# Attention and feed-forward in one kernel on one core: loads reordered, global V rows copied in SBUF, one copy moved to ScalarE

## Chip, cores, metric

The kernel runs on one core of one Trainium2 chip. The metric is device time in microseconds (us). Before the change it is 301.4 us (median; single runs 301.0 to 301.5). A profile is one execution with the hardware profiler; its span, from the first to the last instruction, is about 1.9 us shorter than the time of the same execution. Below, TensorE is PE (PEld its loading of weights), VectorE DVE, ScalarE ACT, GpSimd POOL, SyncE SP.

## The reference

Attention of four batches, eight heads, 768 positions, head dimension 64. A query sees the last 96 keys and the first 8 ("global") keys, with a bias that falls linearly with distance. The result, 3072 rows of 512, goes through a gated feed-forward network with 1536 hidden units. Cut to what matters:

```python
scores = scale * q @ k.T - slope[h] * dist          # dist = 96 for a global key outside the window
a = softmax(where(keep, scores, -1e9))              # keep: global, or 0 <= i - j < 96
x = (a @ v).transpose(0, 2, 1, 3).reshape(B * S, H * D)
g = x @ w_gate
out = (g * sigmoid(g) * (x @ w_val)) @ w_out
```

Inputs and output are float32; what is loaded is kept as fp16, and all the loads that convert are issued from POOL. Below, MB of loads are counted in fp16, as they land.

## The kernel before

Batch 0's attention runs first, alone (the prologue). Then come 8 tiles of 384 tokens; each tile has 12 steps, and each step does one gate and value block of the feed-forward, a quarter of an output block of the tile before, and one of the six steps of a pair of heads of the next batches. The parts that matter:

```python
def load_v(b, c):                  # 7 pieces with 8 rows of room for the global keys in each
    if c < NCH:
        nc.gpsimd.dma_start(out=vS[NG:NG + n, b, c, :, :], in_=v[...])
    else:
        for cc in range(NCH):      # the 8 global rows, once per piece, from DRAM
            nc.gpsimd.dma_start(out=vS[0:NG, b, cc, :, :], in_=v[b, :, 0:NG, :]...)

def transposes(self):              # step 0 of a pair of heads: PE transposes q and k into PSUM
    ...
    nc.scalar.copy(out=self.qT..., in_=trq...)
    for c0, c1, n in (...):        # kT with gaps for the global keys, two instructions
        nc.vector.tensor_copy(out=k3[...], in_=t3[...])
    nc.vector.tensor_copy(out=k3[:, :, 0:NG], ...)
# steps 1 to 3: scores(): matmul, exp on ACT, product with the mask (DVE for batch 0, POOL later)
# steps 4, 5: values(): den and num matmuls, then DVE (batch 0) or ACT, DVE and POOL (later)

stage(0)
load_qk(0, 0, 2); load_qk(0, 2, 4)
for c in range(NCH + 1): load_v(0, c)
load_qk(0, 4, 8)
for g in range(4): load_w(g)
for g in range(3): load_wo(g)
stage(1); load_qk(1, 0, 8)
for c in range(NCH + 1): load_v(1, c)
# ... prologue: batch 0 ...
for t in range(NT):
    for f in range(NFF):
        i = NFF * t + f
        for fn in loads.get(i, []): fn()     # loads of batches 2 and 3
        gate_val(t, f)
        if t > 0: out_part(t - 1, f // 4, f % 4)
        attention(i + AHEAD)                 # AHEAD = 2
```

In the traces POOL's loads stand in program order among its other work. A load issued from POOL takes POOL's time (0.9 us for a large piece of V, see below) and holds back the POOL work behind it.

The softmax here doesn't subtract the row's maximum and nothing guards it: scores larger than these inputs give would overflow.

Of the kernel before, what the change touches and what calls it, by code (L numbers as in the profile page):

```python
# [10 lines left out]
FP16 = mybir.dt.float16  # L11
# [26 lines left out]
def kernel(  # L38
# [12 lines left out]
    nc = tc.nc  # L51

    B, H, S, D = q.shape
    NG, NL = int(n_global), int(n_local)
# [9 lines left out]
    NCH = 7  # L64
# [16 lines left out]
    sb = ctx.enter_context(tc.tile_pool(name="sb", bufs=1))  # L81
# [13 lines left out]
    ones = sb.tile([128, 64], FP16, name="ones")  # L95
    nc.vector.memset(ones, 1.0)
    kTs = [sb.tile([128, NCH * 128], FP16, name=f"kT{i}") for i in range(2)]
    for t in kTs:
        nc.vector.memset(t[:, 6 * 128 + 56:], 0.0)
    vS = sb.tile([128, B, NCH, H, D], FP16, name="vS")  # L100
    nc.vector.memset(vS[:, :, 6, :, :], 0.0)

    qst, kst = {}, {}

    def stage(b):
        qst[b] = sb2.tile([128, H, J * D], FP16, name="qst", tag="qst")
        kst[b] = sb2.tile([128, H, J * D], FP16, name="kst", tag="kst")

    def load_qk(b, h0, h1):
        for st, src in ((qst[b], q), (kst[b], k)):  # L110
            nc.gpsimd.dma_start(  # L111
                out=st[:, h0:h1, :],
                in_=src[b, h0:h1].rearrange("h (p j) d -> p h (j d)", p=128))

    def load_v(b, c):
        if c < NCH:
            n = min(KC, S - KC * c)
            nc.gpsimd.dma_start(  # L118
                out=vS[NG:NG + n, b, c, :, :],
                in_=v[b, :, KC * c:KC * c + n, :].rearrange("h p d -> p h d"))  # L120
        else:
            for cc in range(NCH):
                nc.gpsimd.dma_start(
                    out=vS[0:NG, b, cc, :, :],
                    in_=v[b, :, 0:NG, :].rearrange("h p d -> p h d"))

    wg = sb.tile([128, NC, DFF], FP16, name="wg")
    wv = sb.tile([128, NC, DFF], FP16, name="wv")
# [3 lines left out]
    def load_w(g):  # L132
        f0 = WF * g
        for w, src in ((wg, moe_w_gate), (wv, moe_w_val)):
            nc.gpsimd.dma_start(
                out=w[:, :, f0:f0 + WF],
                in_=src[:, f0:f0 + WF].rearrange("(c p) f -> p c f", p=128))

    def load_wo(g):
        nc.gpsimd.dma_start(  # L140
            out=wo[:, 4 * g:4 * g + 4, :],
            in_=moe_w_out[512 * g:512 * g + 512].rearrange("(f p) d -> p f d", p=128))
# [8 lines left out]
    def bank(name, dt=FP32, cols=512):  # L151
        tags = state["tags"]
        tag = tags[state["n"] % len(tags)]
        state["n"] += 1
        return ps.tile([128, cols], dt, name=name, tag=tag)
# [5 lines left out]
    class Pair:  # L161
# [13 lines left out]
        def transposes(self):  # L175
            b, hp = self.b, self.hp
            trq = bank("trq", FP16, S)
            trk = bank("trk", FP16, S)
            for st, tr in ((qst[b], trq), (kst[b], trk)):
                for j in range(J):  # L180
                    for hi in range(2):
                        nc.tensor.transpose(  # L182
                            tr[64 * hi:64 * hi + 64, 128 * j:128 * j + 128],
                            st[:, 2 * hp + hi, D * j:D * j + D], ident)
            self.qT = sb2.tile([128, S], FP16, name="qT", tag="qT")
            self.kT = kTs[hp % 2]
            nc.scalar.copy(  # L187
                out=self.qT.rearrange("r (p j) -> r p j", j=J),
                in_=trq.rearrange("r (j p) -> r p j", j=J))
            k3 = self.kT.rearrange("r (c m) -> r c m", m=128)  # L190
            t3 = trk.rearrange("r (j p) -> r p j", j=J)
            for c0, c1, n in ((0, 6, KC), (6, 7, S - 6 * KC)):
                nc.vector.tensor_copy(  # L193
                    out=k3[:, c0:c1, NG:NG + n].rearrange("r c (p j) -> r c p j", j=J),
                    in_=t3[:, 20 * c0:20 * c0 + (c1 - c0) * (n // J), :].rearrange(
                        "r (c p) j -> r c p j", c=c1 - c0))
            nc.vector.tensor_copy(  # L197
                out=k3[:, :, 0:NG],
                in_=k3[:, 0, NG:2 * NG].unsqueeze(1).broadcast_to([128, NCH, NG]))
# [22 lines left out]
        def values(self, half, norm):  # L222
            b, hp = self.b, self.hp
            lo, hi_q = HALF[half]
            n_q = hi_q - lo
            num = bank("num")
            den = bank("den")
            parts = []
            for c in range(NCH):
                cb, col, q0, n = chunks[c]  # L230
                a, z = max(q0, lo), min(q0 + n, hi_q)
                if a < z:
                    parts.append((c, cb, col + a - q0, a - lo, z - a))
            for dst, ones_side in ((den, True), (num, False)):
                for i, (c, cb, col, o, n) in enumerate(parts):
                    for hi in range(2):
                        r = slice(64 * hi, 64 * hi + 64)
                        nc.tensor.matmul(  # L238
                            dst[r, o:o + n],
                            lhsT=ones if ones_side else vS[:, b, c, 2 * hp + hi, :],  # L240
                            rhs=self.at[hi, cb][:, col:col + n],
                            start=(i == 0), stop=(i == len(parts) - 1),
                            skip_group_check=True)
            dT = sb2.tile([128, 416], FP32, name="dT", tag="dT")
            dR = sb2.tile([128, 13], FP32, name="dR", tag="dR")
            rb = sb2.tile([128, 416], FP32, name="rb", tag="rb")
            nb = n_q // 32
            nc.vector.transpose(dT[:, 0:n_q], den[:, 0:n_q])
            nc.vector.reciprocal(
                out=dR[:, 0:nb], in_=dT[:, 0:n_q].rearrange("p (n i) -> p n i", i=32)[:, :, 0])  # L250
            nc.vector.transpose(  # L251
                rb[:, 0:n_q].rearrange("p (n i) -> p n i", i=32),
                dR[:, 0:nb].unsqueeze(2).broadcast_to([128, nb, 32]))
            dst = xT[:, hp, b * S + lo:b * S + hi_q]
            if norm == "vector":
                nc.vector.tensor_mul(dst, num[:, 0:n_q], rb[:, 0:n_q])
            else:
                ns = sb2.tile([128, 416], FP32, name="ns", tag="ns")
                nc.scalar.copy(out=ns[:, 0:n_q], in_=num[:, 0:n_q])  # L259
                nc.gpsimd.tensor_mul(dst, ns[:, 0:n_q], rb[:, 0:n_q])  # L260
# [38 lines left out]


    stage(0)
    load_qk(0, 0, 2)
    load_qk(0, 2, 4)
    for c in range(NCH + 1):
        load_v(0, c)
    load_qk(0, 4, 8)
    for g in range(4):
        load_w(g)
    for g in range(3):
        load_wo(g)  # L310
    stage(1)
    load_qk(1, 0, 8)
    for c in range(NCH + 1):
        load_v(1, c)

    pairs = {(b, hp): Pair(b, hp) for b in range(B) for hp in range(NP)}

# [12 lines left out]

    todo = [(b, hp, s) for b in range(1, B) for hp in range(NP) for s in range(6)]
    AHEAD = 2
    loads = {}
    for b in range(2, B):
        base = 24 * (b - 2) + 2
        loads[base] = [lambda b=b: (stage(b), load_qk(b, 0, 8))]
        for c in range(NCH + 1):
            loads.setdefault(base + 1 + c, []).append(lambda b=b, c=c: load_v(b, c))

    def attention(i):  # L340
        if i < len(todo):
# [53 lines left out]
```

## Time and profile before

| | kernel before |
|---|---|
| time, median | 301.4 us |
| span of the profile | 299.3 us |
| end of batch 0 on DVE | 45.4 us |
| first feed-forward step | 57.0 us |
| first step of the second tile | 85.75 us |
| from there to the end | 213.55 us |

The last four rows are read from the timeline; the first three of them are points in time, the fourth is the stretch from the last point to the end of the span. The prediction shows those lines. Two groups of the page show what POOL does beside its mask products. Columns: line, engine, operation, count, then busy time and mean ns of one, then idle time before it and what ended most of it.

```profile
L220 POOL TENSOR_TENSOR at<-at,masks 128x432 f16<-128x432 f16 x72 | 70.5, 1005 | 31.7 <-ACT at L216 31.6
...
L118 POOL DMA_DIRECT2D vS<-in_v_dram x28 | 25.1, 909 | 10.9 <-DMA wo<-in_moe_w_out_dram 4.9
```

Issuing the large V loads costs POOL nearly as much each (0.9 us) as one mask product (1.0 us).

### The profile page before, as it was taken

To read this page: it belongs to the slowest core of one execution; us is meant where nothing else is said; L and a number is where in the kernel's file an instruction comes from. 1 tells how busy PE (TensorE), PEld (TensorE's weight loads), DVE (VectorE), ACT (ScalarE), POOL (GpSimd) and SP (SyncE) were. 2 spreads that over 40 slices of the span, in tenths; PEclk is the share of its full clock that TensorE was granted. 3 is DMA by queue.
4 is the path that set the end of the run, shared out by engine and by line. 5 is a ranking of instruction groups with operands and counts; after the bars stand their busy time and mean duration, and the time that the engine had idled before them with its cause. 6 is when DMAs were issued, how large, how long until landed. Compare 5 with 4: busy or idle time off the path is not lost.

```text
span 299.3 us, 5659 instructions
## 1 busy us (share of the span) xinstructions
PE 256.5 (86%) x2176; PEld 141.5 (47%) x2176; DVE 179.4 (60%) x372; ACT 133.9 (45%) x265; POOL 152.9 (51%) x179
## 2 busy tenths in 40 slices
PE   2528541599799999999999999999999999999983
PEld 1316320245455555555555555555555555555531
DVE  1646990268777576776667666757585755555510
ACT  6826411146365545544555554554546433333311
POOL 8893442399997454979973627272727200000000
PEclk9999755599999999999999999999999999999999
DMA  8989999909950010299501000100010000100111
GB/s 127 123 117 203 204 206 204 130 7 150 146 31 30 7 37 36 23 213 134 64 4 37 36 22 16 37 35 2 36 37 35 2 35 36 37 35 35 37 70 70
DMA packets 48554, 21.30 MB, mean 71 GB/s; under 512 B 31504, under 2 KB 45456, under 8 KB 48528
## 3 DMA queue, kind: packets, MB, share of 16 engines
q0 software_dynamic: 44784, 14.40, 42.9%
q1 hardware_dynamic: 3744, 6.55, 6.0%
q8 instruction: 17, 0.28, 0.4%
q14 instruction: 9, 0.07, 0.1%
HBM read 29.02 MB, written 6.29 MB: 118 GB/s over the span
## 4 chain that ended last, share of the span: by engine, by line
PE 71%; DMA 16%; POOL 8%; DVE 2%; ACT 1%; issue 1%; POOLq 0%; ACTq 0%; DVEq 0%
PE gps L272 21%; PE ops L291 21%; PE vps L272 19%; DMA vS<-in_v_dram 7%; DMA wo<-in_moe_w_out_dram 5%; POOL at L220 3%; DMA wv<-in_moe_w_val_dram 3%; PE scA L210 3%; PE den L238 3%; PE num L238 2%; POOL vS L118 2%; PE trq L182 2%; PE trk L182 1%; POOL qst L111 1%; ACT osb L296 1%
## 5 line engine op out<-in xcount | busy, mean ns | idle before, releaser
L280 DVE SCALAR_TENSOR_TENSOR sl<-th,gps 128x384 f32<-128x384 f32 x96 | 52.9, 551 | 61.3 <-ACT th L278 61.3
L220 POOL TENSOR_TENSOR at<-at,masks 128x432 f16<-128x432 f16 x72 | 70.5, 1005 | 31.7 <-ACT at L216 31.6
L272 PE MATMUL gps<-xT,wg 128*128 128x384 f16 x384 | 79.8, 331 | 0.0
L272 PE MATMUL vps<-xT,wv 128*128 128x384 f16 x384 | 78.8, 328 | 0.0
L291 PE MATMUL ops<-wo,hT 128*128 128x512 f16 x288 | 76.3, 379 | 2.1 <-ACT osb L296 2.1
L278 ACT ACTIVATE th<-gps 128x384 f32<-128x384 f32 x96 | 47.5, 494 | 37.1 <-PE gps L272 36.7
L282 DVE TENSOR_TENSOR hT<-vps,sl 128x384 f16<-128x384 f32 x96 | 53.5, 558 | 10.1 <-PE vps L272 0.2
L272 PEld LDWEIGHTS <-wv 128*128 128x128 f16 x384 | 37.8, 98 | 25.2 <-issue 0.5
L272 PEld LDWEIGHTS <-wg 128*128 128x128 f16 x384 | 32.0, 98 | 27.7 <-issue 4.9
L216 ACT ACTIVATE at<-scA 128x432 f16<-128x432 f32 x48 | 25.5, 532 | 37.9 <-PE scB L210 37.9
L291 PEld LDWEIGHTS <-hT 128*128 128x128 f16 x288 | 28.2, 98 | 27.6 <-issue 3.0
L260 POOL TENSOR_TENSOR xT<-ns,rb 128x352 f16<-128x352 f32 (+1 forms) x24 | 24.1, 1005 | 26.1 <-DVE rb L251 26.0
L118 POOL DMA_DIRECT2D vS<-in_v_dram x28 | 25.1, 909 | 10.9 <-DMA wo<-in_moe_w_out_dram 4.9
L193 DVE COPY kT<-trk 128x720 f16<-128x720 f16 (+1 forms) x32 | 16.3, 551 | 24.0 <-PE trk L182 24.0
L187 ACT COPY qT<-trq 128x768 f16<-128x768 f16 x16 | 12.9, 803 | 30.5 <-PE trq L182 30.5
L296 ACT ACTIVATE osb<-ops 128x512 f32<-128x512 f32 x24 | 14.3, 597 | 25.1 <-PE ops L291 25.1
L216 ACT ACTIVATE at<-scB 128x432 f16<-128x432 f32 x48 | 25.5, 532 | 0.0
L210 PE MATMUL scA<-qT,kT 64*128 64x216 f16 (+2 forms) x112 | 18.7, 267 | 7.9 <-DVE kT L197 5.6
L182 PE MATMUL trq<-ident,qst 128*64 128x128 f16 x192 | 9.7, 246 | 17.4 <-DMA qst<-in_q_dram 17.4
L259 ACT COPY ns<-num 128x352 f32<-128x352 f32 (+1 forms) x24 | 11.5, 479 | 29.0 <-PE num L238 23.5
L238 PE MATMUL den<-at,ones 128*64 128x216 f16 (+4 forms) x256 | 18.8, 260 | 5.1 <-POOL at L220 2.4
L251 DVE STREAM_TRANSPOSE rb<-dR 128x352 f32<-128x352 f32 (+1 forms) x32 | 18.5, 578 | 2.7
(28 smaller groups left out, 177.2 us busy)
## 6 DMA issues: line engine op xcount, KB each, us to landing
out_dram<-osb SPq DMA_DIRECT2D x24, 256.0 KB, 2.0
vS<-in_v_dram POOLq DMA_DIRECT2D x24, 120.0 KB, 7.6
qst<-in_q_dram POOLq DMA_DIRECT2D x3, 768.0 KB, 8.1
kst<-in_k_dram POOLq DMA_DIRECT2D x3, 768.0 KB, 11.6
wg<-in_moe_w_gate_dram POOLq DMA_DIRECT2D x4, 384.0 KB, 11.8
wv<-in_moe_w_val_dram POOLq DMA_DIRECT2D x4, 384.0 KB, 13.0
wo<-in_moe_w_out_dram POOLq DMA_DIRECT2D x3, 512.0 KB, 16.6
vS<-in_v_dram POOLq DMA_DIRECT2D x28, 8.0 KB, 2.1
```

Source lines behind the costliest of these rows:

```text
L118: nc.gpsimd.dma_start(out=vS[NG:NG + n, b, c, :, :], in_=v[b, :, KC * c:KC * c + n, :].rearrange("h p d -> p h d"))
L182: nc.tensor.transpose(tr[64 * hi:64 * hi + 64, 128 * j:128 * j + 128], st[:, 2 * hp + hi, D * j:D * j + D], ident)
L210: nc.tensor.matmul(sc[hi][:, col:col + n], lhsT=self.kT[r, 128 * c:128 * c + 128], rhs=self.qT[r, q0:q0 + n], start=True, stop=True)
L216: nc.scalar.activation(out=at, in_=sc[hi][:, 0:BANK], func=AF.Exp, scale=scale)
L220: mul_eng.tensor_mul(at, at, masks[:, 2 * hp + hi, WIN * bk:WIN * bk + BANK])
L238: nc.tensor.matmul(dst[r, o:o + n], lhsT=ones if ones_side else vS[:, b, c, 2 * hp + hi, :], rhs=self.at[hi, cb][:, col:col + n], start=(i ...
L260: nc.gpsimd.tensor_mul(dst, ns[:, 0:n_q], rb[:, 0:n_q])
L272: nc.tensor.matmul(dst[:, 0:TB], lhsT=w[:, c, 128 * f:128 * f + 128], rhs=xT[:, c, TB * t:TB * t + TB], start=(c == 0), stop=(c == NC - 1))
L278: nc.scalar.activation(out=th, in_=gps[:, 0:TB], func=AF.Tanh, scale=0.5)
L280: nc.vector.scalar_tensor_tensor(out=sl, in0=th, scalar=1.0, in1=gps[:, 0:TB], op0=AluOp.add, op1=AluOp.mult)
L282: nc.vector.tensor_mul(hTs[t][:, f, :], vps[:, 0:TB], sl)
L291: nc.tensor.matmul(ops, lhsT=hTs[t][:, f, 128 * i:128 * i + 128], rhs=wo[:, f, :], start=(f == 0), stop=(f == NFF - 1))
```

## The change

The intent is to begin the feed-forward as soon as batch 0 is done, by loading before it only what it needs at first, and to take work from POOL and DVE. Cut to its core:

```diff
+        nc.sync.dma_start(                       # global V rows: one copy in SBUF, from SP
+            out=t[0:NG, :, :, :],
+            in_=t[NG:2 * NG, 0, :, :].unsqueeze(1).broadcast_to([NG, NCH, H, D]))
-                nc.vector.tensor_copy(
+                (nc.scalar.copy if b == 0 else nc.vector.tensor_copy)(     # kT, two instructions
     stage(0)
+    stage(1)
     load_qk(0, 0, 2)
     load_qk(0, 2, 4)
-    for c in range(NCH + 1):
-        load_v(0, c)
+    load_v(0)
     load_qk(0, 4, 8)
-    for g in range(4): load_w(g)                 # (lines joined here)
-    for g in range(3): load_wo(g)
-    stage(1)
-    load_qk(1, 0, 8)
-    for c in range(NCH + 1): load_v(1, c)
+    load_w(0)
+    load_qk(1, 0, 4)
+    load_w(1)
 ...
+    loads = {0: [lambda: load_v(1)], 1: [lambda: load_w(2)], 2: [lambda: load_w(3)],
+             3: [lambda: load_wo(0)], 4: [lambda: load_wo(1)], 5: [lambda: load_wo(2)],
+             6: [lambda: load_qk(1, 4, 8)]}
     for b in range(2, B):                        # q, k at base, base + 2; V at base + 4
-        base = 24 * (b - 2) + 2
+        base = 24 * (b - 2) + 10
```

One more part of the change, not shown in this cut: the single tile vS for V became four tiles, one for each batch.

More of the change, by code (lines that the diff above doesn't have):

```diff
@@ L99 @@
         nc.vector.memset(t[:, 6 * 128 + 56:], 0.0)
-    vS = sb.tile([128, B, NCH, H, D], FP16, name="vS")
-    nc.vector.memset(vS[:, :, 6, :, :], 0.0)
+    vSs = [sb.tile([128, NCH, H, D], FP16, name=f"vS{b}") for b in range(B)]
+    for t in vSs:
+        nc.vector.memset(t[:, 6, :, :], 0.0)
     qst, kst = {}, {}
@@ L113, in load_qk, with load_v @@
                 in_=src[b, h0:h1].rearrange("h (p j) d -> p h (j d)", p=128))
-    def load_v(b, c):
-        if c < NCH:
+    def load_v(b):
+        t = vSs[b]
+        for c in range(NCH):
             n = min(KC, S - KC * c)
             nc.gpsimd.dma_start(
-                out=vS[NG:NG + n, b, c, :, :],
+                out=t[NG:NG + n, c, :, :],
                 in_=v[b, :, KC * c:KC * c + n, :].rearrange("h p d -> p h d"))
-        else:
-            for cc in range(NCH):
-                nc.gpsimd.dma_start(
-                    out=vS[0:NG, b, cc, :, :],
-                    in_=v[b, :, 0:NG, :].rearrange("h p d -> p h d"))
+        nc.sync.dma_start(
+            out=t[0:NG, :, :, :],
+            in_=t[NG:2 * NG, 0, :, :].unsqueeze(1).broadcast_to([NG, NCH, H, D]))
     wg = sb.tile([128, NC, DFF], FP16, name="wg")
@@ L239, in values @@
                             dst[r, o:o + n],
-                            lhsT=ones if ones_side else vS[:, b, c, 2 * hp + hi, :],
+                            lhsT=ones if ones_side else vSs[b][:, c, 2 * hp + hi, :],
                             rhs=self.at[hi, cb][:, col:col + n],
@@ L301 @@
     stage(0)
+    stage(1)
     load_qk(0, 0, 2)
     load_qk(0, 2, 4)
-    for c in range(NCH + 1):
-        load_v(0, c)
+    load_v(0)
     load_qk(0, 4, 8)
-    for g in range(4):
-        load_w(g)
-    for g in range(3):
-        load_wo(g)
-    stage(1)
-    load_qk(1, 0, 8)
-    for c in range(NCH + 1):
-        load_v(1, c)
+    load_w(0)
+    load_qk(1, 0, 4)
+    load_w(1)
     pairs = {(b, hp): Pair(b, hp) for b in range(B) for hp in range(NP)}
@@ L332 @@
     AHEAD = 2
-    loads = {}
+    loads = {0: [lambda: load_v(1)], 1: [lambda: load_w(2)], 2: [lambda: load_w(3)],
+             3: [lambda: load_wo(0)], 4: [lambda: load_wo(1)], 5: [lambda: load_wo(2)],
+             6: [lambda: load_qk(1, 4, 8)]}
     for b in range(2, B):
-        base = 24 * (b - 2) + 2
-        loads[base] = [lambda b=b: (stage(b), load_qk(b, 0, 8))]
-        for c in range(NCH + 1):
-            loads.setdefault(base + 1 + c, []).append(lambda b=b, c=c: load_v(b, c))
+        base = 24 * (b - 2) + 10
+        loads[base] = [lambda b=b: (stage(b), load_qk(b, 0, 4))]
+        loads[base + 2] = [lambda b=b: load_qk(b, 4, 8)]
+        loads[base + 4] = [lambda b=b: load_v(b)]
     def attention(i):
```

## The prediction

> **What bounds the kernel now.** I read the page's slices first, then the waits of the tensor engine, then the stages, then the timeline of the two busiest stretches. The slices (7.5 us each) show three parts:
>
> ```profile
> PE   2528541599799999999999999999999999999983
> PEclk9999755599999999999999999999999999999999
> DMA  8989999909950010299501000100010000100111
> ```
>
> From slice 11 on PE is full at full clock, so nothing is to be won there. In slices 0 to 7 (60 us) PE is mostly idle, its clock falls to a half, and DMA is busy nearly throughout. What PE waits for in the first 70 us:
>
> ```profile
> PE trq L182 <- DMA qst<-in_q_dram: 17.4, 3, 8.0
> PE trk L182 <- DMA kst<-in_k_dram: 5.0, 3, 3.1
> ```
>
> (total us, times, longest.) It waits for q and k rows: once in batch 0, for heads 4 to 7, and once, the longest, for batch 1. The timeline of the second wait:
>
> ```profile
> 44.82 0.59 DVE L256 TENSOR_TENSOR xT<-num,rb 128x416 f16<-128x416 f32 x1
> ...
> 50.51 0.61 PEld L182 LDWEIGHTS <-qst 128*64 128x64 f16 x12 [8.18 <-DMA qst<-in_q_dram]
> ...
> 54.45 0.61 PEld L182 LDWEIGHTS <-kst 128*64 128x64 f16 x12 [3.33 <-DMA kst<-in_k_dram]
> ...
> 57.00 1.46 PE L272 MATMUL gps<-xT,wg 128*128 128x384 f16 x4
> ```
>
> Batch 0 is finished by VectorE at 45.4 us, but the feed-forward starts at 57.0, because the load queue brings all weights (4.7 MB in fp16) before k of batch 1. I cut the run at these points (columns: stretch, length, PE, PEld, DVE, ACT, POOL busy, clock, DMA, GB/s):
>
> ```profile
> 22.80:45.40 22.60, 13.30 (x186) 10.06 (x186) 19.55 (x48) 8.75 (x17) 9.31 (x11) 0.74 1.29 204
> 45.40:57.00 11.60, 2.17 (x28) 1.35 (x29) 1.13 (x4) 0.80 (x1) 3.04 (x5) 0.50 1.67 186
> 60.90:85.75 24.85, 22.06 (x223) 12.36 (x220) 18.79 (x39) 12.59 (x26) 24.73 (x27) 1.00 0.97 98
> 85.75:235.60 149.85, 149.85 (x1321) 80.81 (x1320) 101.24 (x206) 78.43 (x162) 92.32 (x101) 1.00 0.25 43
> ```
>
> Row 1, batch 0 after its last k has come: VectorE works 19.55 of 22.6 us. Row 2: everybody waits for loads. Row 3, the first feed-forward tile (12 steps, 57.0 to 85.75): POOL is busy 24.73 of 24.85 us, and PE waits for its mask products. Row 4: PE is the bound, without a gap. The proof for row 3 are two lines, the second pair's last mask product on POOL and the matmul it releases:
>
> ```profile
> 79.14 1.97 POOL L220 TENSOR_TENSOR at<-at,masks 128x432 f16<-128x432 f16 x2
> ...
> 81.16 0.32 PE L238 MATMUL den<-at,ones 128*64 128x216 f16 x4 [0.70 <-POOL at L220]
> ```
>
> So time = end of batch 0, or of its waits (E) + first tile (12 steps) + the rest, 299.3 - 85.75 = 213.55 us, which stays.
>
> **What the Trainium skill says.** "DMA: Bandwidth & Descriptors", section "Issuing engines are not separate DMA queues": all DMAs run on the same 16 engines, and another issuing engine saves only the issue time. The trace agrees that this time is not nothing on POOL: 0.92 us for a large V load, 0.58 for a small one, 0.74 to 0.80 for weights. The same page, "Anatomy of one DMA": about 2 us are fixed per DMA; here the 8 KB V loads land after 2.1 us. "TensorE: Matmul & The Clock Gate", Part 1: the clock halves after an idle window and comes back after about 3.4 us of work; here it is 0.50 until 60.6 us, 3.6 us after the feed-forward began at 57.0. Agreed.
>
> **Part 1, order of the loads.** After the change only q, k of batch 0 (1.57 MB), V of batch 0, weight group 0 (0.79), heads 0 to 3 of q, k of batch 1 (0.79) and group 1 (0.79) come before the feed-forward. In the trace V's packets move at about 150 GB/s and the others at 204. The first V loads are all in by 13.4 us now. Now POOL then issues seven 8 KB loads, one by one: each POOL issue waits until the load eight issues before it has landed (the first wo, the 29th, waits for a wg, the 21st), so q, k of heads 4 to 7 are issued only at 15.7 and 16.5, with the DMA nearly idle from 14 to 17.5, and land at 20.9 and 22.8. After the change POOL is through with the large V loads at 10.45, issues q and k at once, and their data follow V without a gap: 0.39 MB / 204 GB/s = 1.93 us each plus 0.7 for completion, so q at 16.1 and k at 18.0, 4.8 us earlier. Then the rest, 2.36 MB / 204 = 11.6 us: all in by about 30 us, long before it is needed. The load wait of row 2 is gone; E is set by compute.
>
> **Part 2, global V rows by a copy in SBUF on SP.** It takes 28 issues of 0.58 us from POOL (7 of them before the feed-forward). The copy must wait for V's first piece, perhaps for all, and takes some 2 us: V is whole at 13.5 to 17 us, against 15.3 now.
>
> **Part 3, kT copy of batch 0 on ScalarE.** VectorE loses 4 x (0.90 + 0.20) = 4.4 us. ScalarE copies qT, 768 columns, in 0.82 us, so I estimate 0.65 + 0.2 = 0.85 us of pitch for the two kT copies. But it runs in order: the first kT now stands between qT and the masks for pair 1, which at present run in the gap (6.55 to 8.29). I followed ScalarE by its pitches (qT 0.69, kT 0.85, two exps 0.84, two masks 1.65): kT of pair 0 to 8.4, masks to 10.05, exps of pair 0's first two blocks to 11.75, qT and kT of pair 1 to 13.3, exps to 14.15, masks to 15.8, exps to 16.65. VectorE then begins its first normalisation at 17.1 instead of 15.7. From there its work is eight normalisations (4 x 1.93 + 4 x 2.14 by the timeline), eight pairs of mask products (0.59) and small copies, 21.25 us, plus 1.2 us waiting for ScalarE, which has to make the masks for pair 3 before an exp, and some tenths: **E = 39.8 us** (now 45.4).
>
> **First tile.** Feed-forward begins at E + 1.6, as kT (1.0 + 0.2, on VectorE here) and the first scores must come (55.35 to 57.0 now): T = 41.4. POOL's first mask product begins at T + 0.65, when the first exp is done. Then, in program order: products 1.95; V of batch 1, 7 x 0.95 = 6.65; products 1.95; w(2) 1.58; products 1.95; w(3) 1.58; norm 0.95, wo 0.74, norm 1.08, two wo 1.48; products of pair 1, 1.95; q, k 1.7; products 1.95 and 1.95. Sum 27.5, so the product that frees pair 1's last values is done at T + 28.1; now it is 81.1 - 57.0 = 24.1. From there three steps remain, 85.75 - 81.16 = 4.6. The tile takes 32.8 us against 28.75: **4 us are given back**, because V and the late weights are issued ahead of mask products that PE needs at once; PE will stand from about T + 5 to T + 11. Later bursts (q, k at steps 10 and 12, V at step 14) fall where the products have more than two steps (2.56 us each) of lead: I find no PE stall there.
>
> **Sum.** 41.4 + 32.8 + 213.55 = 287.75 us of span against 299.3: 11.55 less. 301.45 - 11.55 = **289.9; I say 289.5.**
>
> **The rivals.** (a) The loads were the whole of it and POOL keeps up: E as above, tile 28.75 or less, 285.5 us. Against it: POOL is full in row 3, and the work before the decisive product grows. (b) ScalarE becomes the bound of batch 0: kT copies slower than estimated, or the SP copy keeps V back until after 18 us, so E stays at 42 to 44: 292 to 294 us. For it: ScalarE is busy 10.9 of the first 15 us. (c) The moved loads collide with tile 1 on POOL and bring PE gaps after the first tile: 2 to 4 us more. Against it: row 4 has POOL at 62% and PE gapless, with load bursts in it too. (d) Hidden anyway, within 2%: would need all of the 11.6 us of row 2 to come back; only if (b) and (c) both come.
>
> **Range and chances.** E is known to some 2.5 us, the tile to 2: together about 3.5 up, and as much down. Range 285 to 294. 2% faster is below 295.4: chance 0.91; same 0.08; slower 0.01.
>
> **What would show it.** The first wg matmul at about 41 us, with no wait of trq for q of batch 1; trk of pair 2 released at about 18; first VectorE normalisation at 17; POOL full from T to T + 28 with seven V issues in a row after two products; a PE wait of 4 to 6 us for POOL (at L220) in the third step, smaller ones at steps 3, 8 and 9; step 12 some 33 us after the first; the stretch from there to the end 213 to 214 us. The prediction is wrong if the feed-forward starts after 44 us, if the first tile takes under 29 or over 36 us, or if PE shows gaps after it.

## The result

The changed kernel takes 297.5 us (median of 4 runs, 297.0 to 297.8). The ratio to the kernel before is 0.987, with a 95% interval of 0.9855 to 0.989. Ratios here are the mean time of one kernel's runs over that of the other's in the same rounds, so they are not quite the ratio of the medians quoted. Executions over 1.5% slower than the fastest of the same kernel are left out of the means. The time lies outside the predicted range of 285 to 294 us. The change brings 3.9 us (1.3%) where 11.9 were forecast: clear of noise, but less than 2%, an outcome to which the prediction gave a chance of 0.08.

The slices of the profile after (7.4 us each):

```profile
PE   1556568797699999999999999999999999999983
PEclk9999557799699999999999999999999999999999
DMA  8999009999939701000899010100010000100111
```

The idle stretch is shorter, and in slices 4 and 5 (29 to 44 us) DMA stands still. In slice 10, though, PE has a hole again and its clock drops. The stages of the changed kernel (stretch, length, busy time of PE, PEld, DVE, ACT and POOL with counts, clock, DMA, GB/s):

```profile
19.72:41.40 21.68, 14.37 (x210) 11.05 (x210) 17.68 (x45) 11.07 (x22) 0.00 (x0) 0.76 0.61 96
...
42.96:70.57 27.61, 23.27 (x178) 11.75 (x178) 15.20 (x31) 12.40 (x26) 26.57 (x31) 0.85 1.15 133
70.57:81.49 10.92, 6.96 (x65) 3.71 (x65) 5.43 (x12) 2.29 (x4) 3.47 (x4) 0.72 1.16 178
81.49:231.30 149.81, 149.81 (x1319) 80.72 (x1318) 101.00 (x204) 78.31 (x162) 94.21 (x99) 1.00 0.35 53
```

Batch 0 now ends at 41.4 us and the feed-forward begins at 42.96, which is 14.0 us earlier than before. The first tile takes 38.5 us (42.96 to 81.49) instead of 28.75, so 9.8 us are given back. From there to the end are 213.6 us, as before. So 14.0 - 9.8 = 4.2 us of span are won.

Within the tile, POOL is the bound up to 70.57, where its last mask product for the second pair of heads is done: busy 26.57 of 27.61 us. In the next stretch POOL is idle for two thirds of the time and PE is not full either. The timeline of the changed kernel, POOL first:

```profile
65.13 0.81 POOL L112 DMA_DIRECT2D qst<-in_q_dram  x1
65.93 0.75 POOL L112 DMA_DIRECT2D kst<-in_k_dram  x1
```

and PE:

```profile
71.93 0.81 PE L272 MATMUL vps<-xT,wv 128*128 128x384 f16 x4
75.63 0.85 PE L182 MATMUL trq<-ident,qst 128*64 128x128 f16 x12 [2.88 <-DMA qst<-in_q_dram]
77.56 0.85 PE L182 MATMUL trk<-ident,kst 128*64 128x128 f16 x12 [1.08 <-DMA kst<-in_k_dram]
78.34 1.46 PE L272 MATMUL gps<-xT,wg 128*128 128x384 f16 x4
```

The q and k of heads 4 to 7 of batch 1 were issued at 65.1 and 65.9 us but are there only at 75.6 and 77.5, more than 10 us later. PE waits 4.0 us for them, and then its matmuls run at half clock (four gate matmuls take 1.46 us instead of 0.82) until 82.

### The profile page after: what moved, and what is told of

The parts are those of the page before. It is cut to its first block, busy times and chain, and to the rows that moved or that the text cites. A ratio compares the mean times of both kernels' runs of the same rounds, so it can differ in the third digit from the quotient of the medians.

```text
span 295.1 us, 5628 instructions
## 1 busy us (share of the span) xinstructions
PE 260.5 (88%) x2176; PEld 142.9 (48%) x2176; DVE 176.8 (60%) x367; ACT 137.1 (46%) x273; POOL 140.6 (48%) x157
## 4 chain that ended last, share of the span: by engine, by line
PE 73%; POOL 9%; DVE 7%; DMA 7%; ACT 2%; issue 1%; DVEq 0%; ACTq 0%; POOLq 0%
PE gps L272 21%; PE ops L291 21%; PE vps L272 19%; DMA kst<-in_k_dram 7%; POOL vS L120 4%; PE scA L210 3%; PE den L238 3%; POOL at L220 2%; PE num L238 2%; PE trk L182 2%; PE trq L182 2%; DVE rb L251 1%; DVE xT L256 1%; DVE dT L248 1%; DVE at L220 1%
## 5 line engine op out<-in xcount | busy, mean ns | idle before, releaser
L280 DVE SCALAR_TENSOR_TENSOR sl<-th,gps 128x384 f32<-128x384 f32 x96 | 53.0, 552 | 63.6 <-ACT th L278 63.2
L272 PE MATMUL gps<-xT,wg 128*128 128x384 f16 x384 | 81.1, 335 | 0.0
L272 PE MATMUL vps<-xT,wv 128*128 128x384 f16 x384 | 80.5, 333 | 0.0
L278 ACT ACTIVATE th<-gps 128x384 f32<-128x384 f32 x96 | 47.5, 494 | 39.8 <-PE gps L272 39.3
L282 DVE TENSOR_TENSOR hT<-vps,sl 128x384 f16<-128x384 f32 x96 | 53.6, 558 | 10.3 <-PE vps L272 0.6
L272 PEld LDWEIGHTS <-wv 128*128 128x128 f16 x384 | 38.3, 100 | 26.3 <-issue 2.4
L291 PEld LDWEIGHTS <-hT 128*128 128x128 f16 x288 | 28.2, 98 | 27.6 <-issue 2.9
L216 ACT ACTIVATE at<-scA 128x432 f16<-128x432 f32 x48 | 25.6, 534 | 31.5 <-PE scB L210 31.5
L260 POOL TENSOR_TENSOR xT<-ns,rb 128x352 f16<-128x352 f32 (+1 forms) x24 | 24.0, 1005 | 27.6 <-DVE rb L251 27.6
L120 POOL DMA_DIRECT2D vS<-in_v_dram x28 | 24.5, 895 | 0.0
L248 DVE STREAM_TRANSPOSE dT<-den 128x352 f32<-128x352 f32 (+1 forms) x32 | 18.4, 576 | 3.8 <-PE den L238 3.8
L238 PEld LDWEIGHTS <-ones 128*64 128x64 f16 x256 | 11.7, 120 | 18.2 <-issue 15.1
L210 PEld LDWEIGHTS <-kT 64*128 64x128 f16 x224 | 7.8, 99 | 25.9 <-issue 13.3
```

What stands on the lines that cost most here:

```text
L120: nc.gpsimd.dma_start(out=t[NG:NG + n, c, :, :], in_=v[b, :, KC * c:KC * c + n, :].rearrange("h p d -> p h d"))
L210: nc.tensor.matmul(sc[hi][:, col:col + n], lhsT=self.kT[r, 128 * c:128 * c + 128], rhs=self.qT[r, q0:q0 + n], start=True, stop=True)
L216: nc.scalar.activation(out=at, in_=sc[hi][:, 0:BANK], func=AF.Exp, scale=scale)
L238: nc.tensor.matmul(dst[r, o:o + n], lhsT=ones if ones_side else vSs[b][:, c, 2 * hp + hi, :], rhs=self.at[hi, cb][:, col:col + n], start=( ...
L248: nc.vector.transpose(dT[:, 0:n_q], den[:, 0:n_q])
L260: nc.gpsimd.tensor_mul(dst, ns[:, 0:n_q], rb[:, 0:n_q])
```

## The experiments

Every kernel gave the right result. In the table, "start" is the first feed-forward matmul and "tile" the time from there to the first step of the second tile, both from the timeline of each profile. "Rest" is the span less both.

| run | median us | ratio to before | start | tile | rest |
|---|---|---|---|---|---|
| before | 301.4 | 1 | 57.0 | 28.75 | 213.55 |
| after | 297.5 | 0.987 | 43.0 | 38.5 | 213.6 |
| wo_behind_qk | 290.4 | 0.965 | 42.6 | 32.4 | 213.3 |
| qk_before_ff | 289.7 | 0.962 | 42.4 | 31.5 | 213.3 |
| all_early | 284.05 | 0.943 | 42.1 | 26.2 | 213.3 |
| all_early_again | 284.3 | 0.943 | 42.9 | 26.8 | 213.3 |
| kt_on_vector | 295.6 | 0.9825 | 43.1 | 36.5 | 213.3 |
| small_v_loads | 308.6 | 1.027 | 45.95 | 41.8 | 219.1 |
| before_sbuf_copy | 295.8 | 0.9835 | 53.0 | 27.0 | 213.3 |
| hold_rest | 284.8 | 0.946 | 42.4 | 27.0 | 213.3 |
| all_early_kt_vector_again | 284.9 | 0.946 | 43.6 | 26.3 | 213.3 |
| masks_earlier | 283.6 | 0.943 | 41.5 | 26.4 | 213.35 |
| masks_earlier_again | 283.4 | 0.941 | 41.3 | 26.9 | 213.3 |

### The wait for q and k: place in the queue, or POOL too late?

My theory after the result was that the DMA queue holds 3.15 MB of late weights (two groups and w_out) ahead of those q and k, and at 204 GB/s that is 15.4 us. The rival was that POOL simply reaches the issue too late.

```diff
-             3: [lambda: load_wo(0)], 4: [lambda: load_wo(1)], 5: [lambda: load_wo(2)],
-             6: [lambda: load_qk(1, 4, 8)]}
+             6: [lambda: load_qk(1, 4, 8)],
+             7: [lambda: load_wo(0)], 8: [lambda: load_wo(1)], 9: [lambda: load_wo(2)]}
```

> The changed kernel with only the three wo loads moved from steps 3 to 5 to steps 7 to 9, behind q, k of heads 4 to 7 of batch 1. Theory Q (the lost time is the wait of PE for those q, k, which stand in the DMA queue behind 3.15 MB of late weights at 204 GB/s, some 15.4 us): with only 1.57 MB ahead they land about 68 us and the PE wait of 72.7 to 77.6 us and the cold clock after it are gone; the decisive product on POOL comes 1.5 us earlier too; first tile 30.7 us instead of 38.5, time 289.7 us. Rival P (POOL simply reaches that issue too late, landing follows 10.5 us after issue whatever is ahead): POOL reaches it 2.3 us earlier, landing at 73 and 75 us, time 295 us.

It measured 290.4 us, where the theory said 289.7 and the rival 295. POOL reached the issue at 64.1 us, only 1.0 us earlier than in the changed kernel, and yet PE had no wait for these q and k at all. Its timeline, with no wait at either:

```profile
72.41 0.53 PE L182 MATMUL trq<-ident,qst 128*64 128x128 f16 x12
72.77 0.50 PE L182 MATMUL trk<-ident,kst 128*64 128x128 f16 x12
```

Landing 10.5 us after issue, as the rival had it, would have made PE wait until after 74 us. So what decides is what stands ahead of them in the queue. The tile is 1.7 us longer than I had written (32.4, not 30.7).

The next run leaves the late weights and V in the tile and takes only q and k out of it:

```diff
     load_w(1)
+    load_qk(1, 4, 8)
 ...
-             6: [lambda: load_qk(1, 4, 8)]}
```

> The changed kernel with only the second half of q, k of batch 1 moved from step 6 to before the feed-forward; V of batch 1 and the late weights stay in the first tile. This puts the prediction's own sum to the test without the wait it had left out: start 42.7 us, decisive product on POOL 1.6 us earlier than now (two issues less ahead of it), 26.0 us after the start, three steps of 4.6 us, tile 30.7, rest 213.6: span 287.0, time 289.0 us. Rival (POOL's burst costs nothing, only the q, k wait did): as all_early, 284 us. Rival (the wait was caused by something other than the place of q, k in the queue): 295 us or more.

It measured 289.7 us, against 289.0 expected. So 7.8 us of the changed kernel's time hang on where this one pair of loads is issued: the landing wait, the clock lost behind it, and 1.6 us of POOL. What is left, 289.7 us, is close to the prediction's 289.9, but in part by luck: the start is 1.0 us later than predicted and the tile 1.3 us shorter (31.5 instead of 32.8), because two issues fewer are in it. The rival that POOL's burst costs nothing (284 us) falls.

### All loads before the feed-forward

```diff
     load_w(1)
+    load_v(1)
+    load_qk(1, 4, 8)
+    load_w(2); load_w(3)
+    for g in range(3): load_wo(g)
 ...
-    loads = {0: [lambda: load_v(1)], ... }
+    loads = {}
```

> The changed kernel with V of batch 1, the second half of q, k of batch 1 and all late weights issued from POOL before the feed-forward, behind weight group 1, while POOL is idle (16.7 to 43.7 us) and the DMA queue is empty (30 to 47 us). Theory: POOL has only mask products and norms in the first tile, so no PE wait on POOL and none on q, k: tile 25.4 us (two cold steps included), start unchanged at 43.0, the rest 213.6: span 282, time 284.4 us. Rival (VectorE, at 10.7 us of work per 11.2 us of six ideal steps, or the matmul clock becomes the bound of the tile): tile 29 us or more, time 288 us. If the added traffic delays batch 0, its end moves past 41.4 us.

It measured 284.05 us, and 284.3 when repeated. Its stages:

```profile
42.09:68.30 26.21, 24.36 (x238) 13.37 (x237) 19.28 (x41) 14.58 (x30) 16.92 (x18) 0.95 0.59 96
68.30:281.60 213.30, 207.47 (x1634) 111.31 (x1632) 130.12 (x257) 96.72 (x197) 95.56 (x101) 1.00 0.31 53
```

POOL is busy 16.9 of 26.2 us in the tile and no longer the bound; the waits of PE in this tile name neither POOL nor a DMA. Start is not later than in the changed kernel, although 4.7 MB more were asked for before it. POOL issues these loads between 17 and 40 us, when it has nothing else to do, and the data flow while DMA stood still in the changed kernel. Against qk_before_ff the tile is 5.3 us shorter; against all_early_again, from the same rounds as qk_before_ff, 4.7 us in the tile and 5.3 us in time. That is the price of issuing V and the late weights on POOL ahead of mask products which PE waits for: in the tile of qk_before_ff PE waits 3.6 us for POOL, in those of all_early and all_early_again not at all.

> The kernel of all_early once more, beside the next two, as 1 us is in question between them: 284.0 us.

### The copy of the global V rows in SBUF

Undone in the changed kernel:

```diff
-        nc.sync.dma_start(out=t[0:NG, :, :, :], in_=t[NG:2 * NG, 0, :, :]...)
+        for cc in range(NCH):
+            nc.gpsimd.dma_start(out=t[0:NG, cc, :, :], in_=v[b, :, 0:NG, :]...)
```

> The changed kernel with the global V rows loaded again from DRAM by seven small POOL loads per batch. Theory: q, k of heads 4 to 7 are issued at 15.7 instead of 10.3 us and land about 3.1 us later, which batch 0 takes over; in the first tile POOL has 4.1 us more in front of everything, the q, k wait included: time 297.5 + 7.2 = 304.7 us. Rival (only the early part counts, the tile is bound by q, k in the queue and not by POOL): 300.6 us.

It measured 308.6 us: slower than the kernel before, and 3.9 us more than expected. The start is 3.0 us later, as expected, and the tile 3.3 us longer. The rest is also 5.5 us longer than in the changed kernel, which I had not foreseen. Waits of PE in this run, first in its first tile, then after it:

```profile
PE den L239 <- POOL at L221: 8.4, 3, 6.9
```

```profile
PE den L239 <- POOL at L221: 4.2, 7, 0.7
```

Columns: total, times, longest. Fourteen V loads in a row keep POOL for 10 us where seven keep it for 6.1. With V in one burst per batch, this is more than the lead that the mask products have, even in the later tiles, where 4.2 of the 5.5 us are waits for them. In the changed kernel no such wait is left after the first tile. So without the copy in SBUF the new order is a loss (308.6 us against 301.0 in the same rounds).

The same copy alone, in the kernel before:

```diff
-            for cc in range(NCH):
-                nc.gpsimd.dma_start(out=vS[0:NG, b, cc, :, :], in_=v[b, :, 0:NG, :]...)
+            nc.sync.dma_start(out=vS[0:NG, b, :, :, :], in_=vS[NG:2 * NG, b, 0, :, :]...)
```

> The kernel before with only the seven small V loads per batch replaced by one copy in SBUF from SP; order of loads and kT copy as before. Theory: q, k of heads 4 to 7 and everything behind them are issued some 4.5 us earlier, so k of batch 1 lands about 50 us, the feed-forward begins about 52.6 instead of 57.0; POOL begins its first mask product 0.65 us after that instead of 3.9 us, and its work up to the decisive product (20.1 us) is unchanged: tile 25.4 instead of 28.75 us; sum 7.7 us less: time 293.7 us, better than the whole change. Rival (the wait for loads is set by the bytes, the queue was never idle): 298 us.

It measured 295.8 us, 2.1 more than expected but less than the whole change. Timeline:

```profile
50.43 0.85 PE L181 MATMUL trk<-ident,kst 128*64 128x128 f16 x12 [3.13 <-DMA kst<-in_k_dram]
...
52.98 1.46 PE L271 MATMUL gps<-xT,wg 128*128 128x384 f16 x4
```

The k of batch 1 lands at 50.4 instead of 54.45, as expected: in the kernel before, the small loads kept the queue nearly empty from 14 to 17.5 us. The tile came out at 27.0, not 25.4. So this one part of the change, without any new order, brings 5.1 us (300.9 us before in the same rounds), more than the whole change (3.9 us).

### kT on ScalarE

```diff
-                (nc.scalar.copy if b == 0 else nc.vector.tensor_copy)(
+                nc.vector.tensor_copy(
```

> The changed kernel with the kT copy of batch 0 back on VectorE. Theory: before k of heads 4 to 7 lands (19.7 us) nothing is gained or lost; after it batch 0 runs as in the kernel before, 45.4 - 22.8 = 22.6 us: batch 0 ends at 42.3 instead of 41.4 us, time 298.4 us. Rival 1 (the full 4.4 us of VectorE work counted): 301 us. Rival 2 (ScalarE was the bound, the copy cost time): 296 us or less.

Undone in the changed kernel, it measured 295.6 us, which by the number alone speaks for rival 2. But its single runs go from 294.4 to 297.8, and the profile shows the difference only after the start: start 43.1 against 43.0, tile 36.5 against 38.5. In this profile PE stood idle 2.6 us there instead of 4.0, and its clock did not drop at steps 11 and 12. So this run says that the copy on ACT gains 0.1 us at the start, but its time is blurred by the clock. I repeated it where there is no such wait.

> All loads early, as in the run all_early, with the kT copy of batch 0 back on VectorE. In this base there is no wait for q, k and no loss of clock behind it, which blurred the run kt_on_vector. Theory: the copy on ScalarE frees VectorE, which then waits for ScalarE instead; batch 0 ends at the same time within 0.3 us: time 284.0 us, as all_early. Rival 1 (kT on ScalarE is a loss of 2 us, as kt_on_vector's time says): 282 us. Rival 2 (a gain, hidden there): 285 us or more.

The first try is inconclusive: three runs took 284.4 to 286.5 us (ratio 0.949), and the profiled one 866.8 (see the last section). The second try:

> All loads early, kT copy of batch 0 on VectorE, once more, since the first time its profile fell into an execution of 867 us. Theory (copy on ScalarE gains little, VectorE waits for ScalarE instead): batch 0 ends within 1.0 us of all_early's, time 284 to 285.3 us. Rival (it gains the 4.4 us of VectorE work): 288 us. Rival (it is a loss): 282 us.

It measured 284.9 us against 284.3 for all_early_again in the same rounds. By the profiles, batch 0 takes 22.6 us from its third pair's k transpose (19.39) to its end (42.0) with kT on DVE, and 21.7 us (19.68 to 41.36) with kT on ACT. So the move is worth some 0.9 us of batch 0. The other profiles agree: this stretch takes 22.4 us in kt_on_vector and 21.7 in the changed kernel, all_early and hold_rest. In the times themselves the 0.6 us is not clear of noise (the intervals of the two ratios overlap: 0.9443 to 0.9469 and 0.9411 to 0.9446).

The move takes 4.4 us of work from DVE. Two of its four pairs of heads come before k has landed, when DVE has to wait for k anyway (0.5 us with kT on DVE, 1.1 with kT on ACT). In the stretch after it, between these two runs, DVE's work falls from 19.9 to 18.2 us and its idle time grows from 2.7 to 3.5. The changed kernel's DVE timeline shows the waits:

```profile
21.40 0.18 DVE L197 COPY kT<-kT 128x56 f16<-128x56 f16 x1 [1.86 <-ACT kT L193]
...
25.37 0.81 DVE L220 TENSOR_TENSOR at<-at,masks 128x432 f16<-128x432 f16 x2 [1.07 <-ACT at L216]
```

DVE waits for ACT: for the kT copy itself, which comes as late as k does, and for an exp that stands behind two masks (a wait of 0.9 us of this kind is in the kernel before too). The second wait can be taken away by making those masks one step earlier:

```diff
     for t in range(6 + 2 * (NP - 1)):
+        if t == 5:
+            make_masks(6); make_masks(7)
         for hp in range(NP):
 ...
-                if s == 1 and hp + 1 < NP:
+                if s == 1 and hp + 2 < NP:
```

> All loads early, and the masks of pair 3 made on ScalarE one step earlier, before the exps they now stand in front of. Theory: the 1.07 us in which VectorE waits for an exp behind those masks goes, batch 0 ends 0.8 to 1.0 us earlier, time 283.1 us. Rival (VectorE then waits for another engine): as all_early, 284.0 us.

> All loads early and masks of pair 3 one step earlier, once more beside all_early. Theory: 0.5 to 1.0 us less than all_early, 283.3 us. Rival: no difference.

It measured 283.6 us and then 283.4, the second against 284.3 for all_early_again in the same rounds (the intervals of these ratios overlap too). What DVE waits for an exp between 15 and 42 us, in all_early_again and in masks_earlier_again:

```profile
DVE at L220 <- ACT at L216: 2.7, 2, 1.6
```

```profile
DVE at L220 <- ACT at L216: 1.6, 1, 1.6
```

One wait of 1.1 us is gone. In both profiles batch 0 takes 20.7 us from that k transpose to its end, 1.0 less. This is the fastest version found: 283.4 us, 5.9% less than the kernel before and 4.7% (14.1 / 297.5) less than the changed one.

### The landing of k, heads 4 to 7 of batch 0

The prediction had 18.0 us; the transposes that read it start at 18.9 to 19.7 in the runs with the copy in SBUF and no small loads. Do the loads issued behind it delay it?

```diff
     load_qk(0, 4, 8)
+    hold = sb.tile([1, 8], FP16, name="hold")
 ...                                # in the prologue, at t == 5:
+            nc.gpsimd.tensor_copy(hold, kst[0][0:1, 4, 0:8])
+            load_w(0); load_qk(1, 0, 4); ...          # all that came behind it
```

> All loads early, but POOL issues what comes after q, k of batch 0 only when k of heads 4 has landed (a tiny POOL copy reads it). Tests the step that was 1.7 us off: landing of k, heads 4 to 7. Theory (transfers issued behind share the DMA engines with it and delay its landing): k lands at 18.0 instead of 18.9 to 19.7 us, batch 0 ends about 1 us earlier, 283.0 us. Rival (the landing time is set by issue, V and the transfer itself): k lands at 18.9 or later, time 284.0 us; weights come later in both but still before they are read.

It measured 284.8 us. POOL's small copy was released at 19.14 us, so k was there no earlier than with the loads behind it; nothing is gained, and the theory falls. The windows of this run for 16 to 19 us:

```profile
16.00:17.00 1.00, 0.00 (x0) 0.00 (x0) 0.79 (x3) 0.56 (x2) 0.00 (x0) 1.00 1.30 201
17.00:18.00 1.00, 0.90 (x10) 0.52 (x10) 0.93 (x3) 0.00 (x0) 0.00 (x0) 1.00 0.72 110
18.00:19.00 1.00, 1.00 (x16) 0.61 (x12) 0.89 (x3) 0.72 (x2) 0.00 (x0) 1.00 0.14 28
```

The last column is GB/s. With nothing behind it, the transfer runs out over about 1.5 us, 201, 110, 28 GB/s, and only then is k there. Why it ends so slowly was not tested.

## Why the prediction was wrong

**Right: the bound and the three parts.** The rest stayed at 213.6 us with PE full, as predicted, and at 213.3 to 213.6 in every run but small_v_loads; no gaps came from the later bursts. (That the three parts add up to the span is no finding: "rest" is defined so.) Rival (c) was wrong for the change as it is, but small_v_loads shows how near it was: V bursts of 10 us instead of 6 were enough. Rival (b) was wrong: a pair of kT copies took 0.86 to 0.92 us and batch 0 ended before 42. Rival (a) was wrong for this change: POOL's burst had its price. Rival (d), hidden within 2%, named the outcome but not the way: it asked for (b) and (c) both, and what took back more than was forecast was a wait that no rival named.

**Right: part 2.** q and k of heads 4 to 7 were issued at 10.3 us instead of 15.7. V was ready at 15.8 us, within the 13.5 to 17 stated. The copy turned out to be worth more than the prediction noticed.

**Size off: landing of k.** The step "q at 16.1 and k at 18.0" took 0.7 us for completion; k was there at 19.7 in the changed kernel. The prediction's sum for VectorE had it busy from 17.1 us on, with no wait for k; measured, VectorE was done with its earlier work at 19.5 and waited 1.86 us for kT, until 21.4 (line above). With k at 18.0 kT would have been there at 19.7 (estimate: 18.0 plus the 1.7 us that it took from k to kT). So nearly all of the error of E, 1.6 us (41.4 instead of 39.8), is this term. Why k lands late stays open.

**Right in kind: part 3.** DVE's first normalisation began at 16.94 (predicted 17.1). The wait behind the masks of pair 3 was 1.07 us (predicted 1.2). The direct test puts the gain at 0.9 us for 4.4 us of work moved; the prediction did not give this part a gain of its own.

**Right: POOL's burst.** The decisive product was done 27.6 us after the start, against 28.1 predicted and 24.1 before. PE waited 4.0 us for POOL in the tile, 3.0 of it in the third step, where 4 to 6 had been named. The price of 4 us was real. Without q and k in it, the burst costs 5.3 us (qk_before_ff against all_early).

**The step that failed:** "From there three steps remain, 85.75 - 81.16 = 4.6." It took 10.9 us: 4.0 of the 6.3 us more are waits for q and k, and the rest goes with the half clock behind them (four gate matmuls in 1.46 instead of 0.82 us). The sum for the tile counted what each load costs POOL, 1.7 us for q and k, but not when its data land. I had worked out landing times before the feed-forward and not inside it. The loads of steps 1 to 5 put 3.15 MB into the queue from 53.6 us on. At 204 GB/s this takes 15.4 us, until 69 at the earliest, and 0.79 MB of q and k, 3.9 us more, come behind it: 72.9 at the very best, where PE was ready for them at 72.7. They were there at 75.6 and 77.5; the queue had not been full from the start (34 GB/s between 54 and 56 us). The cause is tested: q and k ahead of w_out, or out of the tile, remove the wait (290.4 and 289.7 us).

The rule of the Trainium skill that applies stands in "DMA: Bandwidth & Descriptors", section "Two DMAs through the same engine are not ordered": within one queue of one DMA engine the descriptors start in order, though their completion is not promised in order. The trace agrees: all of POOL's loads went through one queue (q0), and q and k, issued more than 10 us ahead of their landing, came after all the weights issued before them (the last of these were there by 74.4 us). The prediction used the skill for what an issue costs but not for this.

**A slip in the reading.** Of the three waits for q in the first 70 us (17.4 us) the first, 5.0 us, is the very first load of the run, which the prediction passed over. Nothing in its sum rests on it.

**Sum:** 287.75 predicted; + 1.6 (E) + 5.7 (tile 38.5 instead of 32.8) = 295.05, and the span is 295.1.

## What to carry to other kernels

When a load is moved, write down two times for it: when the issuing engine reaches it, and when its data land behind everything already in the queue. Then compare the second with the step that reads it; a load needed soon must not stand behind loads needed late. Where issuing costs time on an engine that also computes, issue in a stretch where that engine and the queue are both idle: here these loads left no wait for POOL or a DMA in the tile when issued between 17 and 40 us, and the tile was 5 us longer (without q and k) or 12 us longer (with them) when they were issued inside it.

## What the Trainium skill lacked or had wrong

- "DMA: Bandwidth & Descriptors", section "Issuing engines are not separate DMA queues", calls the time to initiate a DMA usually small relative to the DMA itself. That is not contradicted (0.9 us for a V load that took 5.0 us to land), but the section leaves out what mattered here: the 0.6 to 0.95 us per load stand in POOL's own order of work, ahead of its mask products. Issuing V and the late weights inside the tile cost 5.3 us of 289.7 (qk_before_ff against all_early), and fourteen V loads instead of seven cost 11 us in all (small_v_loads against the changed kernel).
- None of the pages that I read says how many DMAs may be under way from one issuing engine. Where a POOL issue waited in these kernels, it was for a load of the kind issued eight earlier (in the kernel before, the first w_out load, the 29th, waited 1.2 us for a gate-weight load; the 21st is one). Whether the chip or the program's semaphores set this was not tested.
- "DMA: Bandwidth & Descriptors", section "Anatomy of one DMA", gives about 2 us fixed per DMA plus bytes at 436 GB/s, and says that most of the 2 us is completion. I took 0.7 us for the end; the two loads of hold_rest ran out over about 1.5 us (201, 110, 28 GB/s) and k was there at 19.1 us. The page's 2 us was nearer than my 0.7. Whether its 436 GB/s holds depends on the bytes that are counted: these loads moved at about 204 GB/s in fp16, twice that in the float32 that is read.
- "TensorE: Matmul & The Clock Gate", Part 1, warns that recorded clock events are unreliable. One execution of all_early_kt_vector is a case to be careful with: 866.8 us, and its trace holds no clock event at all (its page has no PEclk line), so that the clock of 1.00 listed for it was not measured. Its output-projection matmuls took 1102 ns each (last line below), where the page of the kernel before has 379, and PE's weight loads for them 220 ns instead of 98, while VectorE's and ScalarE's instructions took as long as ever (554 ns instead of 551 at L280, 491 instead of 494 at L278). So only PE was slow. The three other runs took 284 to 287 us. It happened in one execution only; whether it was the clock is not shown, and its cause is open.

```profile
L291 PE MATMUL ops<-wo,hT 128*128 128x512 f16 x288 | 260.3, 1102 | 2.1 <-ACT osb L296 2.1
```
